# Two more tiles of attention output transposed by DMA: units 22 and 23 of a fused attention and SwiGLU kernel

## The chip, the cores and the metric

The kernel runs on one core of a Trainium2 chip. The metric is the time of one execution on the device in microseconds, as the median of several runs. A core has five engines that work at the same time, each through its own queue in order: TensorE (PE, matrix products), VectorE (DVE), ScalarE (ACT), GpSimd (POOL) and SyncE (SP, which here only issues DMAs). TensorE writes into PSUM, a small memory in banks, from which VectorE and ScalarE read. All else lies in SBUF, the larger on-chip memory. DMA transfers run on 16 DMA engines that the core has.

## The reference

Two steps follow each other. The first is causal attention in a sliding window of 128 positions with a linear distance bias for each head. It has 8 batches, 8 heads, 576 positions and a head size of 64:

```python
scores = scale * np.matmul(q, k.transpose(0, 1, 3, 2)) + bias     # where 0 <= i - j < 128
attn = softmax(scores)
x = np.matmul(attn, v)                    # 8 x 8 x 576 x 64, as 4608 tokens x 512
```

The second is a gated feed-forward layer on these 4608 tokens, with widths of 512 and 1536:

```python
g, val = x @ w_gate, x @ w_val            # 512 -> 1536
out = (g * sigmoid(g) * val) @ w_out      # 1536 -> 512
```

## The kernel before

**Attention by units.** The attention is cut into 36 units, nine for each pair of batches: four tiles of 128 positions of the one batch, four of the other, and a ninth tile (p = 8) that joins the last 64 positions of both. For a unit, `scores` computes the scores of the unit's keys on TensorE, ScalarE takes the exponential, and VectorE multiplies with the bias mask. `weighted` (L336) multiplies with v on TensorE into two PSUM tiles `av`, and VectorE divides by the sum (`rec`, L359) and writes the result `x` (L360). The pool of `x` has three buffers (L136), so the `x` of a unit is written where that of the unit three before was, once all that reads the older one is done.

**The transposition of x.** The feed-forward layer needs x with its 512 features on the partitions. `x_transposed` (L370) does this for one unit, into a quarter of `xT`, the tile of one block of 512 tokens. Block 5, for example, holds the units 22 to 25. It has two ways. Below `X_DMA_FROM` TensorE multiplies with an identity in four pieces into a PSUM tile `px` (L384), and ScalarE copies it to `xT` (L388; for the first four units VectorE, L386). From `X_DMA_FROM` on SyncE issues one DMA transpose from SBUF to SBUF (L378).

**Feed-forward by blocks.** `ffn` (L716) goes through nine blocks of 512 tokens. Up to block 5, `wide` makes the gate products `pg` and value products `pv` (L412), ScalarE a tanh (L430), and VectorE two products (`uu`, L431, and `hT`, L442). The output product is computed by `strassen` with seven half-size products instead of eight (L547). Its results are read out of PSUM by ScalarE and VectorE (L552 among them) and go out in stores from SyncE (L458). Blocks 6 to 8 compute gate and value by seven products as well (L636). VectorE makes the sums for these schemes (L500 to L503, L610 to L613) in between.

**The inputs.** GpSimd issues the loads of q, k and v, which also cast from 32 to 16 bits (L181, L187). From the eleventh tile of k and q on (`QK_DMA_FROM`), SyncE transposes these by DMA too (L235), into homes `kT` and `qT` that go round 12 and 9 places.

**The order of the work.** `everything` (L982) weaves the two steps: `ffn` yields after each group of products, and after each yield attention advances until its count reaches a target, or until the units that a block needs are done (`ready`, L960, and `lead`, L1002). The order of TensorE's instructions is as the program emits them, throughout. For VectorE, ScalarE and SyncE that holds only up to step 60 (SyncE never); after that a planner orders their queues when the program is built, from its own model of durations. The order of each queue is fixed then[...].

In `attention` (L872) the units from `LATE` = 13 on, as long as TensorE transposes them, are transposed one unit late: `x_transposed` of a unit is called after `weighted` of the next one (`waiting`). A unit that DMA transposes is handed on at once, after what still waits.

Of the kernel before, what the change touches and what calls it, by code (L numbers as in the profile page):

```python
# [16 lines left out]
P = 128  # L17
WIN = 128
QK_DMA_FROM = 11
X_DMA_FROM = 24  # L20
MASKS_AT = (3.0, 5.0, 6.0, 7.0)
ALONE = 8
MANUAL = "compute"
# [5 lines left out]
LEAD = 6  # L29
# [21 lines left out]
def kernel(  # L51
# [68 lines left out]
    def make_mask(n):  # L120
        to, of = ((msk[0][:, :, 0:64], reg[:, :, 128:192]),
                  (msk[1][:, :, 64:128], reg[:, :, 128:192]),
                  (msk[2][0:64, :, 0:64], reg[0:64, :, 0:64]),
                  (msk[2][64:128, :, 64:128], reg[64:128, :, 64:128]))[n]
        nc.scalar.copy(to, of)
# [18 lines left out]
    def busy(n):  # L144

        t_ = ps_f.tile([P, 512], FP32, name="nil", tag="po", bufs=1)
        for _ in range(n):
            nc.tensor.matmul(t_, idle[:, 0:P], idle, start=True, stop=True)
# [221 lines left out]
    def x_transposed(i):  # L370
# [5 lines left out]
        dst = xT[n][:, :, j * P:(j + 1) * P]  # L376
        if i >= X_DMA_FROM:
            nc.sync.dma_start_transpose(dst, x)  # L378
# [458 lines left out]
    def first_tiles():  # L837

        first_masks()
        transposes_to(1)  # L840
        begin_scores(0, 0, 0)
        transposes_to(2)
        begin_scores(0, 0, 1)
        transposes_to(need[0])
        begin_scores(0, 1, 0)
        begin_scores(0, 1, 1)
        begin_scores(1, 0, 0, ps_f, "gv", 3)
        for n, _ in enumerate(run(scores(0))):
            if n == 0:
                begin_scores(1, 0, 1, ps_f, "gv", 3)  # L850
                transposes_to(need[1])
        for i in range(FIRST):
            if i + 1 < FIRST:
                for n, _ in enumerate(run(scores(i + 1))):
                    if n == 0 and i == 0:
                        begin_scores(2, 0, 0)
                        begin_scores(2, 0, 1)
                    if n == 0 and i + 2 < FIRST:
                        transposes_to(need[i + 2])
            else:  # L860
                later_masks()
                for m in range(2):
                    wide(0, m, "g", P)
            weighted(i)
            if 0 < i < FIRST - 1:
                x_transposed(i - 1)
        x_transposed(2)
        begin(4, 2)
        x_transposed(3)
        begin(4, 3)  # L870

    def attention():  # L872
# [5 lines left out]
        for i in range(FIRST, last + 1):  # L878
# [13 lines left out]
            yield i - len(waiting)  # L892
            if late and i < X_DMA_FROM:
                if waiting:
# [64 lines left out]
    done = n_att = 0  # L959
    ready = [4, 8, 13, 17, 22, 26, 31, 35, 36]  # L960

    def att_step():
        nonlocal done, n_att
        r = next(att, None)
        if r is not None:
            done = r
            n_att += 1
        return r is not None
# [7 lines left out]
    def progress(steps):  # L976
        total = 0.0
        for size in steps:
            total += size
            yield total  # L980

    def everything():  # L982
        nonlocal done
        base = 0
        busy(WARM)
        with tc.manual_schedule(engines=ENGINES[MANUAL]):
            first_tiles()
            done = FIRST
            steps = progress(ffn())
            while (at := next(steps)) < ALONE:  # L990
                if at == 2.0:
                    nc.scalar.copy(idm2, idm)
                if at in MASKS_AT:
                    make_mask(MASKS_AT.index(at))
        fixed = ExitStack()
        for step in steps:
            if step >= FIXED_FROM and fixed is not None:
                fixed.enter_context(tc.manual_schedule(engines=ENGINES["pe"]))
                fixed, held = None, fixed
            b1 = 24 + 3 * PRE  # L1000

            lead = LEAD if done < X_DMA_FROM - 2 else LEAD + 4  # L1002
            blk = (0 if step + LEAD < b1 else 1 if step + LEAD < 60
                   else min(NBLK - 1, 2 + int((step + lead - 60) // 34.5)))
            if step < b1:

                target = base + 1.25 * max(0, step - ALONE) + 1.5 * max(0, step - 16)
            elif step < 60:
                target = base + 32 + SECOND * 8 * (step - b1) / (60 - b1)
            else:  # L1010
                target = 84 + (step - 57) * RATE / 34.5
            most = n_att + 2 if step >= 60 else 1000
            while (n_att < min(target, most) or done < ready[blk]) and att_step():
                pass
        held.close()

    everything()
    queue.close()

# [29 lines left out]
```

## Time and profile before

| what | before |
|---|---|
| time, median of 3 runs | 335.95 us (335.81 to 336.2) |
| span of the profiled execution | 333.8 us |
| px products on TensorE (L384) | 96, of 220 ns each |
| copies of px on ScalarE (L388) | 20, of 583 ns each |
| DMA transposes of x (L378) | 12, median of 2.4 us from issue to landing, longest 9.7 us |
| DMA transposes of k and q (L235) | 50, medians of 7.4 and 7.5 us |
| share of the DMA engines' time taken by GpSimd's queue | 89.3% |

The table's counts are of instructions: one unit's px is four products. A line of the profile names the engine, the source line, the operation, and what it writes and reads (`out<-in`). In a listing in order of time the first number is the start in us from the beginning of the span, the second is how long the instruction or the merged group lasts, and a bracket tells of idle time of the engine before it and what ended it. The DMA engines are busy for nearly all of the first half, in tenths of 40 slices of the span:

```profile
DMA  9999999999999999999979952030101101011014
```

### The profile page before, as it was taken

What the parts mean: (1) busy time and instruction counts of PE and PEld (TensorE: products, weight loads), DVE (VectorE), ACT (ScalarE), POOL (GpSimd) and SP (SyncE); (2) the same over time, 40 slices, a digit from 0 to 9 for tenths busy, and PEclk for the clock granted to TensorE, in tenths of its full rate; (3) what the DMA queues carried; (4) which work ended last, traced back from release to release, by engine and by line L of the source; (5) the groups of instructions that cost most, each with busy time, mean ns of one, the idle gap of its engine ahead of it and who ended that gap; (6) DMA issues with size and microseconds to landing.
All of it is one profiled execution on the core that took longest, in us unless ns stands there. A gap on an engine that the chain in (4) does not pass through costs nothing.

```text
span 333.8 us, 7731 instructions
## 1 busy us (share of the span) xinstructions
PE 326.3 (98%) x2963; PEld 218.8 (66%) x2963; DVE 274.2 (82%) x643; ACT 207.9 (62%) x415; POOL 111.1 (33%) x138
## 2 busy tenths in 40 slices
PE   8999999999999999999999999999999999999994
PEld 4664465544466655656655655666788888888884
DVE  4678978999797879987999999999855985775683
ACT  5876776474766667567556465563577667676650
POOL 8967777176774275744035000000000000000000
PEclk9999999999999999999999999999999999999999
DMA  9999999999999999999979952030101101011014
GB/s 152 168 179 177 173 185 151 121 128 155 146 169 148 156 167 176 135 180 136 146 177 135 167 62 81 16 96 16 66 21 43 65 0 66 15 50 63 2 65 127
DMA packets 160581, 37.38 MB, mean 112 GB/s; under 512 B 148384, under 2 KB 156192, under 8 KB 160544
## 3 DMA queue, kind: packets, MB, share of 16 engines
q0 software_dynamic: 118880, 18.62, 89.3%
q1 hardware_dynamic: 40976, 17.64, 29.3%
q10 hardware_dynamic: 688, 0.62, 0.6%
q8 instruction: 23, 0.38, 0.5%
q14 instruction: 14, 0.11, 0.1%
HBM read 37.91 MB, written 9.44 MB: 142 GB/s over the span
## 4 chain that ended last, share of the span: by engine, by line
PE 88%; DVE 6%; ACT 2%; DMA 1%; issue 1%; ACTq 0%; DVEq 0%
PE po L547 19%; PE pg L412 17%; PE pv L412 17%; PE gX L636 9%; PE av L356 5%; PE gY L636 5%; PE ps L288 4%; PE p L547 3%; PE gZ L636 2%; DVE uu L431 2%; PE px L384 2%; PE psc L324 2%; PE po L466 2%; DVE hT L442 1%; PE pt L214 1%; DMA stage<-distance 1%
## 5 line engine op out<-in xcount | busy, mean ns | idle before, releaser
L412 PE MATMUL pv<-xT,wv_sb 128*128 128x512 f16 (+2 forms) x312 | 76.6, 363 | 0.2
L412 PE MATMUL pg<-xT,wg_sb 128*128 128x512 f16 (+2 forms) x324 | 76.5, 355 | 0.1
L430 ACT ACTIVATE tt<-pg 128x512 f16<-128x512 f32 x68 | 40.9, 603 | 44.5 <-PE pg L412 44.0
L294 ACT ACTIVATE ex<-ps 128x512 f16<-128x512 f32 x96 | 50.0, 606 | 6.9 <-PE ps L288 6.9
L431 DVE SCALAR_TENSOR_TENSOR uu<-tt,pg 128x512 f16<-128x512 f16 x67 | 45.6, 681 | 8.9 <-ACT tt L430 8.6
L442 DVE TENSOR_TENSOR hT<-uu,pv 128x512 f16<-128x512 f16 x68 | 46.2, 680 | 1.6
L181 POOL DMA_DIRECT2D va<-in_v_dram x40 | 34.2, 862 | 38.2 <-PE av L356 25.6
L547 PEld LDWEIGHTS <-hT 128*128 128x128 f16 x384 | 37.2, 98 | 10.6 <-issue 0.8
L412 PEld LDWEIGHTS <-wg_sb 128*128 128x128 f16 x324 | 28.6, 98 | 23.5 <-issue 2.2
L412 PEld LDWEIGHTS <-wv_sb 128*128 128x128 f16 x312 | 27.7, 98 | 24.3 <-issue 2.4
L187 POOL DMA_DIRECT2D kn<-in_k_dram x39 | 33.4, 860 | 15.6 <-DMA qT<-qn 7.4
L187 POOL DMA_DIRECT2D qn<-in_q_dram x39 | 33.4, 864 | 13.8 <-DMA va<-in_v_dram 8.3
L547 PEld LDWEIGHTS <-S 128*128 128x128 f16 x288 | 27.4, 98 | 7.3 <-issue 1.4
L300 DVE TENSOR_TENSOR ex<-ex,m_reg 128x1024 f16<-128x1024 f16 x42 | 28.5, 684 | 3.0 <-ACT ex L294 3.0
L360 DVE TENSOR_TENSOR x<-av,rec 128x256 f16<-128x256 f32 x72 | 28.6, 419 | 0.5
L547 PE MATMUL po<-T,S 128*128 128x256 f16 x192 | 25.9, 273 | 0.3 <-ACT u2s L573 0.3
L547 PE MATMUL po<-T,hT 128*128 128x256 f16 x192 | 26.0, 273 | 0.0
L328 ACT ACTIVATE exc<-psc 128x512 f16<-128x512 f32 x40 | 21.4, 606 | 2.7 <-PE psc L324 2.6
L690 DVE TENSOR_TENSOR hT<-s,v 128x512 f16<-128x512 f16 x18 | 7.6, 424 | 17.7 <-ACT s L689 17.7
L356 PEld LDWEIGHTS <-ex 128*128 128x128 f16 x384 | 17.5, 97 | 4.4 <-issue 1.0
L356 PE MATMUL av<-va,ex 128*128 128x65 f16 x384 | 19.3, 193 | 0.3 <-ACT ex L294 0.3
L288 PE MATMUL ps<-qT,kT 64*128 64x256 f16 x192 | 16.0, 272 | 0.5 <-DVE qT L219 0.3
(129 smaller groups left out, 535.4 us busy)
## 6 DMA issues: line engine op xcount, KB each, us to landing
out_dram<-osb SPq DMA_DIRECT2D x32, 256.0 KB, 2.8
va<-in_v_dram POOLq DMA_DIRECT2D x32, 128.0 KB, 8.3
qn<-in_q_dram POOLq DMA_DIRECT2D x31, 128.0 KB, 8.8
kn<-in_k_dram POOLq DMA_DIRECT2D x31, 128.0 KB, 8.9
wg_sb<-in_moe_w_gate_dram POOLq DMA_DIRECT2D x6, 256.0 KB, 7.7
wo_sb<-in_moe_w_out_dram POOLq DMA_DIRECT2D x3, 512.0 KB, 8.0
wv_sb<-in_moe_w_val_dram POOLq DMA_DIRECT2D x5, 256.0 KB, 8.1
kn<-in_k_dram POOLq DMA_DIRECT2D x8, 64.0 KB, 8.4
```

The source lines that it names most:

```text
L181: nc.gpsimd.dma_start(va[rank][p0:p1, :, 0:D], src)
L187: nc.gpsimd.dma_start(t_[p0:p1], src)
L288: nc.tensor.matmul(two[par][:, j, :], kT[rows, ks, pair, :], qT[rows, p:p + 2, pair, :], start=(j == 0 and not early_tile), stop=(j == 1))
L294: nc.scalar.activation(e[:, o:o + 2, :], banks[q4][par], AF.Exp, scale=scale)
L356: nc.tensor.matmul(av[:, j, :], w, val, start=(n == 0), stop=(n == len(todo) - 1))
L360: nc.vector.tensor_mul(x[:, 4 * half:4 * half + 4, :], av[:, :, 0:D], rec.broadcast_to([P, 4, D]))
L412: nc.tensor.matmul(ps[:, c0:c1], w[:, kb, ms], xT[n][:, kb, c0:c1], start=(kb == 0 and c0 == 0), stop=(kb == NKB - 1 and c1 == 512), skip_ ...
L430: nc.scalar.activation(tt, pg[:, c0:c1], AF.Tanh, scale=0.5)
L431: nc.vector.scalar_tensor_tensor(out=uu, in0=tt, scalar=one if (n, m) == PIN else 1.0, in1=pg[:, c0:c1], op0=ALU.add, op1=ALU.mult)
L442: nc.vector.tensor_mul(hT[n][:, m, c0:c1], acted[(n, m)][1][:, c0:c1], pv[:, c0:c1])
L547: nc.tensor.matmul(dst, a[:, m, cols], b[:, m, :], start=(start and m == 0), stop=(m == HM - 1), skip_group_check=True)
L636: nc.tensor.matmul(dst[:, i, :], w[:, kb, c0 + i * P:c0 + (i + 1) * P], a[:, kb, :], start=(start and i == 0 and kb == 0), stop=(i == 1 an ...
```

## The change

Units 22 and 23, the first two of block 5, are transposed by DMA, as units 24 on are, and no longer by TensorE and ScalarE. This takes eight products and two copies from these engines and two PSUM tiles from their pool. `lead`, which had been tied to the constant, keeps the value 22, so that the order in which TensorE's work is woven doesn't change otherwise.

```diff
@@ -17,7 +17,7 @@
 QK_DMA_FROM = 11
-X_DMA_FROM = 24
+X_DMA_FROM = 22
 MASKS_AT = (3.0, 5.0, 6.0, 7.0)
@@ -999,7 +999,7 @@
-            lead = LEAD if done < X_DMA_FROM - 2 else LEAD + 4
+            lead = LEAD if done < 22 else LEAD + 4
             blk = (0 if step + LEAD < b1 else 1 if step + LEAD < 60
```

## Prediction

> **What bounds the kernel now.** I read the busy shares first, then the engines by stretches of time, then TensorE, VectorE and SyncE in order of time around units 22 and 23.
>
> ```profile
> PE 326.3 (98%) x2963; PEld 218.8 (66%) x2963; DVE 274.2 (82%) x643; ACT 207.9 (62%) x415; POOL 111.1 (33%) x138
> ```
>
> TensorE (PE) is busy for 98% of the span. The ends of matmuls are modelled, so I also look at VectorE (DVE), by stretches (the columns are PE, PEld, DVE, ACT and POOL busy, clock, DMA, GB/s):
>
> ```profile
> 140.00:159.00 19.00, 19.00 (x179) 11.81 (x177) 15.78 (x35) 12.25 (x26) 9.11 (x11) 1.00 1.98 152
> 159.00:167.00 8.00, 8.00 (x75) 4.69 (x73) 8.00 (x21) 4.06 (x9) 0.00 (x0) 1.00 1.94 144
> 167.00:193.00 26.00, 25.97 (x230) 15.30 (x229) 25.23 (x64) 14.32 (x30) 7.59 (x10) 1.00 1.70 161
> 193.00:240.00 47.00, 46.95 (x400) 29.02 (x399) 46.58 (x116) 25.51 (x52) 0.00 (x0) 1.00 0.21 55
> ```
>
> From 159 us to 240 us DVE works without a pause but for 1.19 us (0.77 before 193, 0.42 after). Here two engines bound the kernel together: PE has no gaps, and DVE has no time to catch up. Now the two transposes that go, on PE:
>
> ```profile
> 153.85 1.03 PE L412 MATMUL pg<-xT,wg_sb 128*128 128x512 f16 x4
> 154.71 0.39 PE L384 MATMUL px<-idm,x 128*128 128x128 f16 x4
> 154.94 1.03 PE L412 MATMUL pv<-xT,wv_sb 128*128 128x512 f16 x4
> ```
>
> A group lasts 0.39 us, but the next starts 0.23 us after it (154.94 - 154.71; for unit 23 161.06 - 160.84 = 0.22). That step is its price. The unit numbers follow from the counts: 20 copies of L388 are units 4 to 23, the 12 DMA transposes of L378 are 24 to 35, and the last px (160.84) is unit 23. Then DVE, where x is written (L360):
>
> ```profile
> 147.68 0.42 DVE L360 TENSOR_TENSOR x<-av,rec 128x256 f16<-128x256 f32 x1
> ...
> 148.22 0.42 DVE L360 TENSOR_TENSOR x<-av,rec 128x256 f16<-128x256 f32 x1
> ...
> 167.18 0.76 DVE L360 TENSOR_TENSOR x<-av,rec 128x256 f16<-128x256 f32 x2
> ```
>
> The first two are unit 22, the third line is unit 25. There are three x buffers (L136), so unit 25 is written where unit 22 was. Last SyncE, whose queue issues the DMA transposes:
>
> ```profile
> 149.68 1.22 SPq L235 DMA_TRANSPOSE qT<-qn  x1
> 153.14 1.27 SPq L235 DMA_TRANSPOSE kT<-kn  x1
> 154.50 1.21 SPq L235 DMA_TRANSPOSE qT<-qn  x1
> 158.55 5.34 SPq L235 DMA_TRANSPOSE kT<-kn  x2
> 163.99 3.62 SPq L235 DMA_TRANSPOSE qT<-qn  x2
> 167.70 1.00 SPq L458 DMA_DIRECT2D out_dram<-osb  x2
> 168.81 1.23 SPq L235 DMA_TRANSPOSE qT<-qn  x1
> 170.14 1.21 SPq L235 DMA_TRANSPOSE kT<-kn  x1
> 171.44 1.22 SPq L378 DMA_TRANSPOSE xT<-x  x1
> ```
>
> SyncE runs far behind. Between 144 and 165 us it waits 10.7 us, in four waits, for k tiles that GpSimd loads; those loads take 12 to 14.4 us to land here. So the two stores of 167.70 issue what was ready at 145.8 (L552, started 145.38) and 147.7 (L588, started 147.28): 20 to 22 us late. The first x transpose (unit 24, whose x is done at 161.7) goes out at 171.44, 10 us late. Nobody suffers: its buffer is written again only at 179.79.
>
> [...] a k transpose whose data is late holds finished stores behind it. [...] a DMA transpose lands 8.7 us after issue at 153.14, under the loads, and 2.4 to 2.5 us at 168.81 and 171.44, when they have drained. [...]
>
> **Part by part.** *Removed on PE:* two groups, 0.23 + 0.22 = 0.45 us. The first can reach the end: before 158.7 DVE still waits for others now and then (0.36 us at 157.44, 0.56 us at 158.70), so it would move along. The second falls where DVE has no gap; PE waits for DVE at 184.33 already (the read of the product's bank, L552, 183.86 + 0.42 = 184.28, releases it). So the gain is 0.23 to 0.45 us if nothing else changes. *Removed on ACT:* two copies of 583 ns. ACT waits for PE between its groups (1.88 us before 161.04), so nothing. Two PSUM tiles fewer only loosen PE. The `lead` line keeps its 22, and PE's own order is the trace order without the two groups.
>
> *Added on SyncE and the DMA engines:* two transposes of some 1.2 us of issue each (1190 to 1240 ns in the L378 and L235 rows). Block 5, which reads them, begins near 200 us, so as data they are in time. K and q transposes are issued more than 20 us before their scores, so a delay of 2.5 us there costs nothing.
>
> *Added wait, the part that counts:* DVE's write of unit 25 now waits until unit 22's DMA transpose has landed; before, it waited for PE's px at 154.71, long past. When does that transpose go out? SyncE's order is fixed at build by a planner. Read against the moments when sources are ready and homes are free on PE, the order seen is sorted: q of rank 32 (home free at 144), stores (145.8, 147.7), q of rank 33 (home free at 150.4), k of rank 33 (156.5), x of unit 24 (161.7), stores (163.0, 165.9), x of unit 25 (167.9). So the planner believes that loads come early, and places everything else by its own readiness. Unit 22's x is ready at 148.64: behind the second store and ahead of q of rank 33. Unit 23's (ready 154.8) follows that q. On the chip this place comes up only when the late k loads are through, at 168.7, and these times do not depend on the change.
>
> So: issue at about 168.8, landing 2.4 to 2.5 us later (the two rows nearest in time), 171.25. DVE reaches the write at 167.18 and stands for 171.25 - 167.18 = 4.1 us, with everything behind it. PE stops soon: the second half of the scores that start at 168.72 needs the PSUM banks that this write frees (at 167.94 before, at 172.0 now, some 3 us later than PE needed them); the next gate product needs the bank read by L442 (167.86, now 171.9 + 0.68), 3.35 us late; at 184.33, where PE had no slack, it is the full 4.1. DVE has 0.1 us to make up (0.77 us idle from 167 to 193, 0.67 us of it the pause that ends at 193.07), and that pause itself ends with PE's product, which is as late. From there PE is dense to the end. The sum is +4.0 us; the 0.45 us saved on PE vanish, since the end of the stall hangs on SyncE and the loads. Unit 23's transpose, at about 171.4, lands by 174 to 176, before unit 26's write (173.58 + 4.1 = 177.7). Bounds for the stall: 1.8 us, if it is planned ahead of the two q at 163.99 and lands 5 us after issue; 5.7 us, if behind q and k of rank 33.
>
> **Rivals and chances.** *Forecast*, a stall of about 4 us: 335.95 + 4.0 = 339.95, chance 0.66. *A longer stall* (behind rank 33, or unit 26 stalls as well): +5.3 to 5.7, 341.4, chance 0.09. *A shorter one* (ahead of the stores or of the late q): +1.8 to 3, near 338, chance 0.09. *No stall* (planned ahead of a k transpose that waits, for instance into SyncE's idle 150.9 to 153.1): the PE saving alone, 335.5 to 335.7, chance 0.16; for it speaks that SyncE has 10.7 us idle there, against it that in the trace no store or x ready at such a time is placed so early. Within this case DVE's order, also planned, may shift by a few tenths either way: of the 0.16 I give 0.05 to faster by over 0.2% (0.67 us), 0.09 to the same, 0.02 to slower. Slower in all is 0.66 + 0.09 + 0.09 + 0.02 = 0.86. The range leaves out the case without a stall (0.16) and holds the others: 336.9 (a stall of 1.8 us less what slack there is) to 341.6.
>
> **What would show it.** Right: on VectorE, one idle stretch of about 4 us before an L360 at 167, released by the DMA of xT; on SyncE, 14 x transposes, the first at about 168.8, directly behind the two stores; PE idle of 3 to 4 us between 168 and 185, none of note later; px 88 times. Wrong: the first x transpose before 158 us and no DVE gap at 167 (then 335.6), or a DVE gap that PE doesn't follow.

## The result and the profile after

The changed kernel takes 340.08 us (median of six runs, 337.12 to 342.43), before takes 336.07 us (six runs). The ratio is 1.0106, with a 95% interval of 1.006 to 1.0153: slower by about 1.1%. The medians of all six runs differ by 4.0 us. The profiled run is the slowest of the six (342.43 us, a span of 340.7 us); the ratio leaves it out, since it is over 1.5% above the fastest, and without it the median is 339.58 us, 3.5 us above before. What its profile shows is therefore looked for again in other runs below; the times that are compared there are medians.

The first view is SyncE's queue in order of time (start, duration, line, what is written and read):

```profile
154.14 1.19 SPq L235 DMA_TRANSPOSE kT<-kn  x1
155.44 1.21 SPq L235 DMA_TRANSPOSE qT<-qn  x1
159.68 5.61 SPq L235 DMA_TRANSPOSE kT<-kn  x2
165.39 3.11 SPq L235 DMA_TRANSPOSE qT<-qn  x2
168.60 1.00 SPq L458 DMA_DIRECT2D out_dram<-osb  x2
169.69 1.23 SPq L378 DMA_TRANSPOSE xT<-x  x1
171.03 1.21 SPq L235 DMA_TRANSPOSE qT<-qn  x1
172.33 1.22 SPq L378 DMA_TRANSPOSE xT<-x  x1
173.65 1.21 SPq L235 DMA_TRANSPOSE kT<-kn  x1
174.94 1.22 SPq L378 DMA_TRANSPOSE xT<-x  x1
```

The transpose of unit 22 stands directly behind the two late stores, that of unit 23 behind the next q. Unit 22's x was done at 148.95 (its second half starts at 148.53 and takes 0.42); its transpose goes out 20.7 us later. The next view is VectorE, the writes of x of units 24 and 25:

```profile
160.40 0.41 DVE L360 TENSOR_TENSOR x<-av,rec 128x256 f16<-128x256 f32 x1
...
161.39 0.42 DVE L360 TENSOR_TENSOR x<-av,rec 128x256 f16<-128x256 f32 x1
...
172.51 0.76 DVE L360 TENSOR_TENSOR x<-av,rec 128x256 f16<-128x256 f32 x2 [5.54 <-DMA xT<-x]
```

Before, unit 25's x started at 167.18 with no pause. Here VectorE stands for 5.54 us, and what releases it is the DMA into xT. That everything behind this write stands still with it was the author's estimate in the forecast; here it is measured, with VectorE busy for 0.00 us from 167 to 171. TensorE follows:

```profile
168.48 0.39 PE L288 MATMUL ps<-qT,kT 64*128 64x256 f16 x4
172.99 0.93 PE L288 MATMUL ps<-qT,kT 64*128 64x256 f16 x4 [4.13 <-DVE x L360]
173.91 1.86 PE L412 MATMUL pg<-xT,wg_sb 128*128 128x512 f16 x4
...
179.40 1.03 PE L412 MATMUL pg<-xT,wg_sb 128*128 128x512 f16 x4
```

The scores stop half way, for want of the PSUM banks that this x frees. And the four gate products behind them last 1.86 us, where four of the same shape last 1.03 us at 179.40. The stretches of the same run tell why (PE, PEld, DVE, ACT and POOL busy, the granted clock of TensorE, DMA, GB/s):

```profile
167.00:169.00 2.00, 1.87 (x14) 0.89 (x12) 0.00 (x0) 1.02 (x3) 0.00 (x0) 1.00 1.64 84
169.00:171.00 2.00, 0.00 (x0) 0.00 (x0) 0.00 (x0) 0.99 (x2) 0.00 (x0) 1.00 1.17 329
171.00:173.00 2.00, 0.01 (x1) 0.01 (x1) 0.49 (x2) 0.00 (x0) 0.00 (x0) 0.76 0.77 171
173.00:175.00 2.00, 2.00 (x7) 0.68 (x8) 2.00 (x5) 1.09 (x2) 0.00 (x0) 0.50 0.38 78
175.00:177.00 2.00, 2.00 (x6) 0.73 (x5) 2.00 (x6) 0.60 (x1) 0.00 (x0) 0.50 0.59 119
177.00:179.00 2.00, 2.00 (x29) 1.64 (x28) 2.00 (x6) 0.00 (x0) 0.00 (x0) 0.53 0.88 300
179.00:181.00 2.00, 2.00 (x17) 1.42 (x15) 1.87 (x7) 0.48 (x1) 1.71 (x2) 1.00 0.17 30
```

From about 172 to 179 us the clock is at half. Busy times hide this: PE is busy for 2.00 of 2 us in the stretches at half clock as in the last one at full clock.

### The profile page after: what moved, and what is told of

It is laid out like the page before. It is cut to its first block, busy times and chain, and to the rows that moved or that the text cites. A ratio compares the mean times of both kernels' runs of the same rounds, so it can differ in the third digit from the quotient of the medians.

```text
span 340.7 us, 7719 instructions
## 1 busy us (share of the span) xinstructions
PE 328.5 (96%) x2955; PEld 219.1 (64%) x2955; DVE 274.1 (80%) x643; ACT 207.2 (61%) x413; POOL 111.0 (33%) x138
## 4 chain that ended last, share of the span: by engine, by line
PE 73%; DVE 18%; ACT 3%; issue 2%; DMA 2%; ACTq 0%; DVEq 0%; SPq 0%
PE po L547 16%; PE pg L412 13%; PE pv L412 12%; PE gX L636 9%; PE gY L636 5%; PE av L356 4%; DVE uu L431 4%; DVE hT L442 4%; PE ps L288 3%; PE p L547 3%; PE gZ L636 2%; DVE x L360 2%; DVE ex L300 2%; PE po L466 2%; PE px L384 2%
## 5 line engine op out<-in xcount | busy, mean ns | idle before, releaser
L412 PE MATMUL pv<-xT,wv_sb 128*128 128x512 f16 (+2 forms) x312 | 77.5, 366 | 0.3 <-DVE uu L431 0.2
L412 PE MATMUL pg<-xT,wg_sb 128*128 128x512 f16 (+2 forms) x324 | 77.3, 358 | 0.1
L430 ACT ACTIVATE tt<-pg 128x512 f16<-128x512 f32 x68 | 40.9, 602 | 47.6 <-PE pg L412 47.6
```

What stands on the lines that cost most here:

```text
L412: nc.tensor.matmul(ps[:, c0:c1], w[:, kb, ms], xT[n][:, kb, c0:c1], start=(kb == 0 and c0 == 0), stop=(kb == NKB - 1 and c1 == 512), skip_ ...
L430: nc.scalar.activation(tt, pg[:, c0:c1], AF.Tanh, scale=0.5)
```

## The experiments

Theory 1 is the forecast's: the time is one wait, of unit 25's x on unit 22's transpose, which goes out late because SyncE's queue is behind. Theory 2, the rival: the time comes from more work on the DMA engines and SyncE, or from the order of VectorE's queue, which the planner did change from about 164 us on. Each ratio is to the kernel before on the same chip.

**Four buffers for x.** One buffer of the reciprocals makes room for it:

```diff
-    xpool = ctx.enter_context(tc.tile_pool(name="xp", bufs=3))
+    xpool = ctx.enter_context(tc.tile_pool(name="xp", bufs=4))
-            rec = xpool.tile([P, 4, 1], FP32, name="rec", tag="rec", bufs=4)
+            rec = xpool.tile([P, 4, 1], FP32, name="rec", tag="rec", bufs=3)
```

> After, with four x buffers instead of three; 32 bytes are taken from the reciprocals (three buffers of them instead of four). The queues of VectorE, ScalarE and SyncE are the same, instruction by instruction. Theory 1 (the time is the wait of unit 25's x on the late DMA transpose of unit 22): no pause of VectorE before the x written near 167 us, although that transpose still goes out at 168 to 170 us; 335.4 to 335.9 us. Theory 2 (the time comes from more DMA work or from the new order that the planner gave VectorE): still 338 us or more.

Measured: 335.41 us, ratio 0.9976 (0.9965 to 0.9986). SyncE is as late as ever, and VectorE doesn't care; first SyncE, then VectorE:

```profile
166.39 1.53 SPq L458 DMA_DIRECT2D out_dram<-osb  x2
168.01 1.23 SPq L378 DMA_TRANSPOSE xT<-x  x1
```

```profile
166.85 0.76 DVE L360 TENSOR_TENSOR x<-av,rec 128x256 f16<-128x256 f32 x2
```

Unit 25's x is written 1.2 us before unit 22's transpose is even issued. The queues of VectorE, ScalarE and SyncE are those of the changed kernel, instruction by instruction, and so is the DMA work. Theory 2 is out, and in this kernel the transposition by DMA is worth having: 0.62 us less than before.

**The control for the buffers.** The same two lines in the kernel before.

> Before, with the same four x buffers and three of the reciprocals: the control for the four buffers. All queues as before. Both theories: 335.8 to 336.3 us, within 0.1% of before.

Measured: 336.27 us, ratio 1.0003 (0.9994 to 1.0011). Four buffers alone do nothing.

**Unit 23 alone by DMA.**

```diff
-X_DMA_FROM = 22
+X_DMA_FROM = 23
...
-        if i >= X_DMA_FROM:
+        if i >= 24 or i == 23:
```

> Only unit 23 by DMA, unit 22 by TensorE again. Its transpose will be queued behind the two late stores and one q transpose, issue near 170 us and land near 172.5; unit 26 takes its buffer at about 173.5. Theory 1: no pause, or one under 0.5 us: 335.5 to 336.3 us. Theory 2 (cost in proportion to transposes moved, or a new VectorE order): half of the loss or more, 338 us.

Measured: 336.03 us, ratio 0.9995 (0.9987 to 1.0004). No x waits for a DMA in its trace. The unit saves 0.22 us of TensorE, which is too little to be told from nothing in these times. VectorE's queue in this trace is already that of the changed kernel, so its new order by itself costs nothing that shows here.

**Unit 22 alone by DMA.**

```diff
-        if i >= X_DMA_FROM:
+        if i >= X_DMA_FROM and i != 23:
             nc.sync.dma_start_transpose(dst, x)
```

> Only unit 22 by DMA, unit 23 by TensorE, three x buffers. Theory 1: unit 22's transpose is the one that comes too late, so the whole loss is here: a pause of VectorE of 2.5 to 5.5 us before the x near 167 us, 338.5 to 341 us. Theory 2 (in proportion to transposes): half of it, 337 to 338 us.

Measured: 340.48 us (339.75 to 340.86), ratio 1.0121 (1.0104 to 1.0138): the whole loss, from one of the two units. (Unit 23 is not transposed one unit late here: its products start at 155.09, and at 160.84 in the kernel before.) VectorE, then two stretches with the clock as before:

```profile
171.28 0.76 DVE L360 TENSOR_TENSOR x<-av,rec 128x256 f16<-128x256 f32 x2 [3.97 <-DMA xT<-x]
```

```profile
173.00:175.00 2.00, 2.00 (x7) 0.70 (x5) 2.00 (x5) 1.11 (x3) 0.00 (x0) 0.55 0.42 89
175.00:177.00 2.00, 2.00 (x28) 1.53 (x27) 2.00 (x5) 0.00 (x0) 0.00 (x0) 0.60 0.99 320
```

**The changed kernel again,** for its spread.

> The changed kernel itself again, on the same chip, since its times spread from 337 to 342 us. Theory 1: the pause of VectorE differs from run to run with the landing of the late k loads, 3 to 6 us; [...] so 337 to 343 us. Theory 2: a spread of the same kind in the kernels that have the same DMAs, four buffers or not.

Measured: 339.99 us (338.52 to 340.45), ratio 1.0114 (1.0096 to 1.0132); the expected 337 to 343 us was the author's estimate. Its profiled run is the shortest, 338.52 us; SyncE, VectorE and TensorE:

```profile
156.41 5.73 SPq L235 DMA_TRANSPOSE kT<-kn  x2
162.25 2.51 SPq L235 DMA_TRANSPOSE qT<-qn  x2
164.85 1.00 SPq L458 DMA_DIRECT2D out_dram<-osb  x2
165.95 1.93 SPq L378 DMA_TRANSPOSE xT<-x  x1
```

```profile
170.00 0.76 DVE L360 TENSOR_TENSOR x<-av,rec 128x256 f16<-128x256 f32 x2 [2.70 <-DMA xT<-x]
```

```profile
170.48 0.72 PE L288 MATMUL ps<-qT,kT 64*128 64x256 f16 x4 [1.29 <-DVE x L360]
```

The k tiles came some 3 us sooner in this run (156.41 against 159.68), and the pause is 2.70 us instead of 5.54. TensorE's longest stop is 1.29 us, and its clock stays at 1.00 in every stretch of this part. Between these two profiles, then, the spread has two sources: when the loads land, and whether TensorE's stop brings its clock down.

**SyncE in program order.** From step 60 on SyncE's queue too is written as the program emits:

```diff
-ENGINES = {"all": None, "compute": {ET.PE, ET.DVE, ET.Activation}, "pe": {ET.PE}}
+ENGINES = {"all": None, "compute": {ET.PE, ET.DVE, ET.Activation}, "pe": {ET.PE, ET.SP}}
```

> After, with SyncE's queue too in the order in which the program emits (from step 60 on), so that unit 22's transpose stands ahead of the k tiles of ranks 29 to 32. Three x buffers; VectorE's queue is the same. Theory 1: it goes out near 150 us, no pause of VectorE near 167; 335.3 to 335.9 us. If the lateness came from the DMA engines and not from the place in the queue, the pause would stay: 338 us or more.

Measured: 335.48 us, ratio 0.9981 (0.9974 to 0.9988), with three buffers. SyncE and VectorE:

```profile
146.53 2.19 SPq L458 DMA_DIRECT2D out_dram<-osb  x2
149.42 1.30 SPq L378 DMA_TRANSPOSE xT<-x  x1
150.81 1.50 SPq L235 DMA_TRANSPOSE kT<-kn  x1
```

```profile
167.34 0.76 DVE L360 TENSOR_TENSOR x<-av,rec 128x256 f16<-128x256 f32 x2
```

The transpose goes out at 149.42, as soon as its x is there (149.36), and the write at 167.34 has no pause before it. So the lateness was the place in the queue and not the DMA engines, which carry the same loads here.

**The control for SyncE's order,** in the kernel before.

> Before, with SyncE's queue in the order in which the program emits: the control. Nothing waited for SyncE before, and k and q are needed long after: both theories 335.7 to 336.5 us.

Measured: 336.14 us, ratio 0.9999 (0.9991 to 1.0007).

**Work of no use ahead of the pause.** Twelve products more in one value product (block 4, first tile), overwritten by the right ones:

```diff
-        for kb in range(NKB):
+        for kb, f in 12 * [(0, 1)] * ((n, m, which) == (4, 0, "v")) + [(kb, 0) for kb in range(NKB)]:
             nc.tensor.matmul(ps[:, c0:c1], w[:, kb, ms], xT[n][:, kb, c0:c1],
-                             start=(kb == 0 and c0 == 0), stop=(kb == NKB - 1 and c1 == 512),
+                             start=(kb == 0 and c0 == 0), stop=bool(f or kb == NKB - 1 and c1 == 512),
```

> After, with 12 products more on TensorE, of no use, ahead of the value product just before the pause (2.6 us of work; their results are overwritten). The planner places VectorE's sums a little differently for it. If the halved clock comes from TensorE's standing still, the clock stays at 1.0 in every run, and the added work is paid by the pause: 338 to 340 us, not 342. If the clock falls for another reason, low clocks and times above 341 us remain, or the 2.6 us come on top: 342 us or more.

Measured: 340.89 us (339.97 to 341.23), ratio 1.0132 (1.0113 to 1.015). The first half held: the mean clock is 0.997 to 1.000 in all four runs, against 0.992 to 1.000 in the four with unit 22 alone by DMA on the same chip, three of which are at 0.995 or below. The second half is a miss, in that the kernel is no faster. In its profiled run (339.97 us) VectorE pauses for 2.84 us, and TensorE then waits for VectorE in other places, 1.13 us in the longest:

```profile
177.86 1.02 PE L412 MATMUL pv<-xT,wv_sb 128*128 128x512 f16 x4 [1.13 <-DVE uu L431]
```

The added work also moved VectorE's planned order, so what the half clock costs can't be read from this kernel.

**More units by DMA, as a better kernel.** First both remedies together:

> Four x buffers and SyncE in program order together, units from 22 on by DMA. Each alone took the pause away, so together nothing more is to be gained: 335.3 to 335.6 us.

Measured: 335.28 us, ratio 0.9981 (0.9974 to 0.9988), as expected. With both remedies, `X_DMA_FROM = 18`:

> The same, and units 18 to 21 (block 4) by DMA too. Each takes some 0.22 us of TensorE; if TensorE bounds there, 4 x 0.22 = 0.9 us less: 334.5 to 334.8. If VectorE bounds the stretch from 125 to 160 us, half of that or nothing: 335.0 to 335.5. If the place of the transposes in the queue brings a wait back, a pause of VectorE before an x, or of TensorE at the start of block 4 (near 165 us), and over 336 us.

Measured: 335.11 us, ratio 0.9974 (0.9966 to 0.9982): 0.17 us less than from 22 on, a fifth of the 0.9 us of TensorE work, and with intervals that overlap. The third of the expected cases did not come. The time lies in the range of the second; whether VectorE is what bounds there was not measured. With both remedies, `X_DMA_FROM = 13`:

> The same, from unit 13 on by DMA: nine units more than from 22. At 0.22 us each 2.0 us less, 333.5 us, if TensorE bounds; block 3 needs units 13 to 16 near 128 us, under the heaviest loads, so a wait of TensorE there of some us is as likely: then 336 us or more.

Measured: 334.21 us (333.98 to 335.63), ratio 0.9956 (0.9941 to 0.9971), the fastest of all kernels here, 1.75 us under before. It lies between the two cases expected: 1.07 us less than from 22 on, where 2.0 us would be all of the TensorE work. No x and no start of a block waits for a transpose in its profile. Last, four buffers with the planner's order of SyncE, `X_DMA_FROM = 18`:

> Four x buffers, the planner's order of SyncE, units from 18 on by DMA. The transposes will be issued 10 to 20 us late, but with four buffers that is covered (a buffer is written again some 25 us later) and block 4 starts 20 us after its last x: no pause, 334.5 to 335.2 us. A pause before the x of units 22 to 25 would show that the lateness is above 20 us.

Measured: 342.57 us (341.78 to 344.09), ratio 1.0205 (1.0182 to 1.0227). A clear miss. SyncE's x transposes of units 18, 19 and 20, then VectorE's x of units 23 and 24:

```profile
137.00 1.22 SPq L378 DMA_TRANSPOSE xT<-x  x1
...
151.70 1.22 SPq L378 DMA_TRANSPOSE xT<-x  x1
...
161.34 1.22 SPq L378 DMA_TRANSPOSE xT<-x  x1
```

```profile
159.59 0.76 DVE L360 TENSOR_TENSOR x<-av,rec 128x256 f16<-128x256 f32 x2 [5.61 <-DMA xT<-x]
...
169.07 0.42 DVE L360 TENSOR_TENSOR x<-av,rec 128x256 f16<-128x256 f32 x1 [2.60 <-DMA xT<-x]
```

I had counted the delay of issue, 20 us, against the 25 us until a buffer is written again, and left out the landing. Unit 19's x was done at 130.8 (130.05 + 0.76), its transpose was issued at 151.70 and released VectorE 7.9 us later, at 159.59: 28.8 us in all. VectorE was ready to write there again at 153.98 (159.59 - 5.61), so that four buffers cover some 23 us; it is the same wait as in the changed kernel, one buffer further.

## Why the prediction was right

**The cause.** The wait named in the forecast is the one that took the time: it goes away with one more buffer (335.41 us), goes away with another place in the queue at the same three buffers (335.48 us), comes whole with unit 22 alone (340.48 us) and not with unit 23 alone (336.03 us). The controls show that neither the buffer nor SyncE's order does anything in the kernel before (336.27 and 336.14 us).

**The place in the queue** was read off right: behind the two stores, ahead of the q of rank 33, unit 23's behind that q. That the planner orders by its own readiness, with loads believed early, was an inference from the queue of before; the queue of after agrees in all three places.

**The size of the pause.** I put the issue at 168.8, the landing 2.4 to 2.5 us later, and so a pause of 4.1 us. The profiles of the repeat, of unit 22 alone and of the changed kernel give 2.70, 3.97 and 5.54 us. The issue came at 165.95, 168.66 and 169.69, and the release 4.05, 2.62 and 2.82 us after it (170.00 - 165.95, and so on). That SyncE's times do not depend on the change was right, but I took those of one run for fixed: they move by about 4 us between runs, with the loads. The middle one of these pauses is near the forecast.

**The step from the pause to the end.** Forecast: the whole pause, and no more. VectorE's queue is the same in the kernel with four buffers, which has no pause, so the last write of x can be compared. The four lines are from four profiles: four buffers, the repeat, unit 22 alone, and the changed kernel.

```profile
225.84 0.41 DVE L360 TENSOR_TENSOR x<-av,rec 128x256 f16<-128x256 f32 x1
```

```profile
229.00 0.41 DVE L360 TENSOR_TENSOR x<-av,rec 128x256 f16<-128x256 f32 x1
```

```profile
230.97 0.43 DVE L360 TENSOR_TENSOR x<-av,rec 128x256 f16<-128x256 f32 x1
```

```profile
232.92 0.42 DVE L360 TENSOR_TENSOR x<-av,rec 128x256 f16<-128x256 f32 x1
```

The last three come 3.16, 5.13 and 7.08 us later than the first. Of this, 0.41, 0.42 and 0.08 us were there before the pause (the write of x before it starts at 161.31, 161.72, 161.73 and 161.39). So the pause and what followed it cost 2.75, 4.71 and 7.00 us, for pauses of 2.70, 3.97 and 5.54 us. In the repeat, where the clock stayed at 1.00, the loss is the pause, as forecast. In the other two, where it fell, 0.7 and 1.5 us came on top, as far as one profile of each can tell. This term was missing from my sum. In the median of six runs something offset it, a shorter pause in other runs or the saving on TensorE; which, the runs do not show. In this the closeness of 339.95 to 340.08 is partly luck.

**The saving on TensorE.** Forecast: 0.23 to 0.45 us without a stall, and lost in it. Without the stall the gain is 0.6 to 0.7 us in the medians (335.41 against 336.03, 335.48 against 336.15), with intervals that begin at 0.4 us. The profiles tell it apart: from the start of ScalarE's first tanh (L430) to that of its last there pass 206.07 us before, 205.73 with unit 23 alone by DMA, and 205.51 with four buffers. Of the gain of 0.56 us, 0.24 is there once unit 22's products are gone and 0.46 once unit 23's are, by the same tanh at 158.5 and 165.0 us. So the second group's 0.22 us reached the end too, although the forecast left it to a VectorE without a gap. The rest, 0.10 us, comes between 167 and 177 us, with unit 23 alone as well; whether VectorE's new order makes it wasn't separated.

**Unit 23, the k and q tiles, block 5:** no wait, as forecast.

## What to carry to other kernels

A transfer that replaces an engine's work takes that engine's promptness away from the buffer it reads. Ask when the old reader let the buffer go and when the new one will: its turn in the issuing queue, behind everything that waits there, plus its landing under load, against the time until the buffer is written again. Here that sum was 21 to 24 us against 18 us with three buffers, and 29 against 23 with four; and a store that goes out 20 us after its data was ready, in the profile before, gave the answer in advance.

## What the hardware showed beyond that

In two of the profiles a stop of TensorE had a price beyond its length. In the changed kernel it stopped for 4.1 us, and the granted clock was at half from 172.05 us on for 6.83 us. With unit 22 alone it stopped for 2.6 us, and a little later for 0.20, and the clock was at half from 173.19 on for 3.41 us. After a stop of 1.3 us, in the repeat, it stayed at 1.00.

The fall did not come at the same point of the stop. With unit 22 alone the clock fell 1.4 us after TensorE had started again (171.77); in the changed kernel it fell 0.9 us before that (172.99). What decides when it falls, and for how long, was not shown: no run here moves a stop to test it.

A DMA transpose of the same 128 by 512 tile landed 2.4 us after issue in the median of the 12 in the kernel before. With four buffers unit 19's released VectorE 7.9 us after its issue, while GpSimd's loads ran (GpSimd is busy for 3.01 of the 5 us from 155 to 160).
